# Attention and two expert stages in one kernel: the gate product of the first stage's weights on four column strips, the low parts of w_in on POOL

## The chip, the cores and the metric

The kernel runs on one core of one Trainium2 chip. The metric is device microseconds (us) of that core, from the first to the last instruction of one launch with what lies around it. Three runs of the kernel before gave 736.51, 736.69 and 737.07 us (median 736.69).

The engines are TensorE (PE, its weight loads are PEld), VectorE (DVE), ScalarE (ACT), GpSimd (POOL) and SyncE (SP, which here only issues DMAs). Each works through its own list of instructions in order.

## The reference

All arrays are float32, except that `moe_w_in` and `moe_w_out` (scaled by a float64 number) come as float64.

```python
# attention: q, k, v are (4, 12, 448, 64)
scores = cap * np.tanh(scale * (q @ k.transpose(0, 1, 3, 2)) / cap)
attn = np.exp(scores - scores.max(-1, keepdims=True))
x = (attn / (attn.sum(-1, keepdims=True) + 1e-9)) @ v      # -> (1792, 768)
# first expert stage: w_in (768, 1024), w_out (1024, 768)
h = x @ w_in
solu = h * softmax(h)
ln = (solu - mean(solu)) / np.sqrt(var(solu) + 1e-6) * g_ln
x = ln @ w_out
# second: each row goes to one of 8 experts
logits = x @ w_gate + modality_bias[modality_id]           # w_gate (768, 8)
e = argmax(logits); gate_w = softmax(logits)[e]
out = gate_w * (relu(x @ w1[e]) @ w2[e])
```

## The kernel before

**Early phase.** The 4 x 12 heads are taken as 24 pairs of heads, and a pair as two *units*, so that unit u is half u mod 2 of pair u // 2 (`unit(n, cp)`, L920). In a unit PE makes the scores of two key chunks (`sc`, L740), ACT takes their tanh (L747) and exp (L752), and PE multiplies the exponentials of the unit before with v (`av`, L782) and adds up their sums on four column strips of the array (`S`, L788). A "column strip" is a quarter of the 128 columns of PE's array: a matmul whose stationary operand has 32 columns can be put on one of four.

**Weights of the first expert stage.** Beside this, in units 0 to 13, two blocks of weights a unit are converted: 16 blocks of w_out (128 x 384, chunk c = 0 to 7, half hf = 0, 1) and 12 of w_in (128 x 512, chunk k = 0 to 5). Units 0 to 11 take one of each, units 12 and 13 two of w_out. DVE puts the float64 halves together to float32 with three integer operations (L481 to L483). Then each weight is split into a rounded high part and a low part, since the products run as three passes (high x high, high x low, low x high):

- w_in: ACT casts the high part (`winh`, L518), DVE subtracts it from the whole (`winl`, L519).
- w_out: DVE scales by g_ln for the high part (`wouh`, L533) and for the low part (`woul`, L534).

**Gate columns.** `wouh`/`woul` carry eight more columns: w_out times w_gate, so that the logits come out of the same product. For that, PE transposes each half block (`pt`, L542), ACT copies the transpose out (`wT`, L545), and PE multiplies: six accumulating matmuls with a 128 x 128 piece of `wT` as stationary operand and 8 gate columns moving (`po`, L552). ACT writes the high part of the 128 x 8 result (L553), DVE the low part (L554, the "gate" step).

**What sets the order.** For the first 8 pairs the order of PE, ACT, DVE and SP is that of the code; POOL's is left to a scheduler. Steps are put off in lists that `unit` empties at fixed places (`flush`): `pe` behind the scores, `cast` (the casts of w_in) behind it, `gate` and `sub` behind each conversion on DVE. PSUM tiles `sc`, `pt`, `po`, `h`, `lt`, `y` share three slots (`atile`), so a tile waits until the tile that had its slot three tiles before is read. Float32 blocks (`ti`, `to`) share four slots, raw blocks four.

In the unit that holds `po` of chunk c, PE runs `sc`, `po`, `pt` (c+1, half 0), `av`, `S`; in the next `sc`, `pt` (c+1, half 1), `av`, `S`. The later phase (from pair 8) runs the two expert stages among the remaining attention; its functions are not touched.

Of the kernel before, what the change touches and what calls it, by code (L numbers as in the profile page):

```python
# [22 lines left out]
P = 128  # L23
# [64 lines left out]
def attn_moe_kernel(ctx, tc, qt, kt, vv, w_in, w_out, packed, ids, mbias, w1, w2, out):  # L88
# [17 lines left out]
    cap_t, g_t = pk[:, 0:1], pk[:, 1:1 + NF]  # L106
    wg_t = pk[:, 1 + NF:].rearrange("p (d w) -> p d w", w=NE)
    sc8 = con.tile([P, 1], F32, name="sc8")
# [5 lines left out]
    bias_t = con.tile([P, NTILE, NE], F32, name="bias_t")  # L114
    mhalf = con.tile([P, 16], F32, name="mhalf")[:, :1]
    lg = con.tile([P, NTILE, NE], F32, name="lg")
    gidx = con.tile([P, NG], I32, name="gidx")
# [9 lines left out]
    ga0 = edge.tile([P, 8], F32, name="ga0")[:, :2]  # L127
    nmx = con.tile([P, NTILE], F32, name="nmx")
    gar = con.tile([P, 80], F32, name="gar")
# [342 lines left out]
    def atile(nm):  # L472
        clock.take(nm)
        return psA.tile([P, 2, 512], F32, tag="A", name=nm)
# [9 lines left out]

    later = {"pe": [], "cast": [], "gate": [], "sub": []}

    def flush(kind):
        fs, later[kind] = later[kind], []
        for f in fs:
            f()  # L490
# [18 lines left out]
    def conv_in(k, hf):  # L509
        raw = rawof[True, k, hf]  # L510
        t = mp.tile([P, 512], I32, tag="x3", name=f"ti{k}_{hf}", bufs=4)
        f64_to_f32(t, raw)
        conv_load()
        tf = t.bitcast(F32)
        h_, l_ = winh[k][:, hf * 512:(hf + 1) * 512], winl[k][:, hf * 512:(hf + 1) * 512]

        def cast():
            act.copy(h_, tf)  # L518
            later["sub"].append(lambda: dve.tensor_sub(l_, tf, h_))  # L519

        later["cast"].append(cast)
# [3 lines left out]
    def conv_out(c, hf):  # L525
# [10 lines left out]
        later["pe"].append(lambda: conv_tr(c, hf))  # L536

    def conv_tr(c, hf):
        tf = wT[c, hf]
        pt = atile(f"pt{c}_{hf}")[:, 0, :]  # L540
        for i in range(3):
            pe.transpose(pt[:, i * P:(i + 1) * P], tf[:, i * P:(i + 1) * P], ident)  # L542
        if hf == 0:
            wT[c] = mp.tile([P, YW], F32, tag="ys", name=f"wT{c}", bufs=1)[:, :DM].rearrange("p (a b) -> p a b", b=P)
        act.copy(wT[c][:, 3 * hf:3 * hf + 3, :], pt[:, :3 * P].rearrange("p (a b) -> p a b", a=3))  # L545
        if hf:
            later["pe"].append(lambda: conv_og(c))

    def conv_og(c):
        po = atile(f"po{c}")[:, 0, :]  # L550
        for i in range(ND):
            pe.matmul(po[:, :NE], wT[c][:, i, :], wg_t[:, i, :], start=(i == 0), stop=(i == ND - 1))  # L552
        act.activation(wouh[c][:, DM:YW], po[:, :NE], AF.Copy, scale=g_t[:, c:c + 1])  # L553
        later["gate"].append(lambda: dve.scalar_tensor_tensor(  # L554
            woul[c][:, DM:YW], po[:, :NE], g_t[:, c:c + 1], wouh[c][:, DM:YW], op0=ALU.mult, op1=ALU.subtract))

# [363 lines left out]
    def unit(n, cp):  # L920
        (b, p), u = pairs[n], 2 * n + cp
        a_scp(b, p, cp)
        flush("pe")
        flush("cast")
        early = plain(b, p) and b > 0
        if early and p and not cp:
            flush("gate")
            finish(b - 1, 4 * p)
        a_exp(b, p, cp)
        if early:  # L930
            if p or cp:
                flush("gate")
                flush("sub")
            if not p or cp:
                finish(b - 1, 4 * p + 2 * cp)
        if cp == 0 and n:
            a_av(*pairs[n - 1], chunks=(2, 3))
        elif cp:
            a_av(b, p, chunks=(0, 1))
        fill(FW[0])  # L940
        if b > 0 and not plain(b, p):
# [8 lines left out]
        flush("gate")  # L950
        flush("sub")
        if u == 3:
# [728 lines left out]
```

## Time and profile before

| | |
|---|---|
| median of 3 runs | 736.69 us |
| profiled execution: its time, its span | 736.02 us, 734.2 us |
| granted TensorE clock (mean share of full) | 0.998 |
| PE, DVE, ACT, POOL busy (share of span) | 98%, 60%, 53%, 14% |
| HBM traffic over the span | 131 GB/s |

The profile's numbers are of one execution of 736.02 us, 0.67 us below the median; the span leaves 1.8 us around it. PE is called busy while a matmul is under way, also one that waits in the array; which engine sets the pace in a stretch is read from the waits and the chain. In the early phase, up to some 75 us, DVE, ACT and PE are each busy more than nine tenths of the time, POOL not at all.

### The profile page before, as it was taken

The numbers are of one execution on the slowest core, as the hardware profiler recorded it, in microseconds if no ns is written. First come the engines' busy times: TensorE is split into PE (matmuls) and PEld (weight loads), VectorE is DVE, ScalarE is ACT, GpSimd is POOL, SyncE is SP. The second block draws the span as 40 slices with busy tenths as digits, with TensorE's granted clock in tenths as the row PEclk, the third lists the DMA queues.
The fourth block names the chain that finished last, engine by engine and source line by source line (L and its number), as shares of the span: only waits on it lengthen the run. The fifth ranks groups of instructions, "written<-read, shape, count | busy, mean of one in ns | idle before, by whom it ended". The sixth has DMA issues, their size and how long they took to land.

```text
span 734.2 us, 11333 instructions
## 1 busy us (share of the span) xinstructions
PE 722.2 (98%) x4310; PEld 558.0 (76%) x4310; DVE 438.0 (60%) x785; ACT 387.6 (53%) x536; POOL 103.9 (14%) x187
## 2 busy tenths in 40 slices
PE   8999999999999999999999999999999999999996
PEld 3443557567767778677778999899879998799995
DVE  7999656647666566565366645857246173473632
ACT  7999756775575554665541224345155162553522
POOL 2000101111031020220030311023110220002011
PEclk9999999999999999999999999999999999999999
DMA  8777221121121110110002202488937359673640
GB/s 277 229 246 242 75 63 50 52 64 44 50 85 38 59 60 13 60 35 13 22 1 105 69 23 79 138 277 305 408 115 262 141 169 393 241 234 141 223 163 25
DMA packets 34354, 97.15 MB, mean 132 GB/s; under 512 B 4647, under 2 KB 10933, under 8 KB 34290
## 3 DMA queue, kind: packets, MB, share of 16 engines
q1 hardware_dynamic: 30578, 79.27, 31.9%
q0 software_dynamic: 3568, 16.83, 6.2%
q8 instruction: 36, 0.59, 0.3%
q10 hardware_dynamic: 144, 0.23, 0.1%
q14 instruction: 28, 0.23, 0.1%
HBM read 85.24 MB, written 11.27 MB: 131 GB/s over the span
## 4 chain that ended last, share of the span: by engine, by line
PE 85%; DVE 6%; ACT 2%; issue 2%; DMA 1%; POOL 1%; POOLq 1%; SPq 0%; another core or an unknown queue 0%; DVEq 0%; ACTq 0%
PE av L782 9%; PE sc L740 8%; PE h L598 6%; PE h L599 5%; PE h L601 5%; PE y L654 5%; PE y L657 5%; PE y L655 4%; PE poD L1389 3%; PE poD L1391 3%; PE poD L1390 3%; PE phD L1286 3%; PE phD L1288 3%; PE phD L1287 3%; PE lt L634 1%
## 5 line engine op out<-in xcount | busy, mean ns | idle before, releaser
L747 ACT ACTIVATE e<-sc,sc 112x896 f32<-112x896 f32 x96 | 94.4, 1004 | 57.7 <-PE sc L740 57.6
L752 ACT ACTIVATE e<-e,pk 112x896 f32<-112x896 f32 x96 | 98.2, 1046 | 1.7
L782 PE MATMUL av<-e,v 112*64 112x448 f32 x384 | 82.8, 552 | 0.9 <-DMA v<-in_vv_dram 0.9
L654 PE MATMUL y<-wouh,lh 128*128 128x392 f32 (+1 forms) x224 | 77.7, 347 | 0.0
L655 PE MATMUL y<-woul,lh 128*128 128x392 f32 (+1 forms) x224 | 75.9, 339 | 0.0
L657 PE MATMUL y<-wouh,ll 128*128 128x392 f32 (+1 forms) x224 | 71.5, 339 | 0.2 <-DVE ll L644 0.2
L598 PE MATMUL h<-winh,xh 128*128 128x512 f32 x168 | 68.9, 410 | 0.0
L599 PE MATMUL h<-winl,xh 128*128 128x512 f32 x168 | 65.8, 392 | 0.0
L601 PE MATMUL h<-winh,xl 128*128 128x512 f32 x168 | 61.2, 391 | 0.0
L782 PEld LDWEIGHTS av<-e,v 112*64 112x64 f32 x384 | 23.4, 136 | 36.5 <-issue 33.7
L654 PEld LDWEIGHTS y<-wouh,lh 128*128 128x128 f32 x224 | 42.0, 188 | 8.4 <-issue 7.1
L1230 DVE TENSOR_TENSOR wl_D<-raw_D,wh_D 128x768 fp32r<-128x768 f32 (+1 forms) x28 | 29.9, 1072 | 27.9 <-ACT wh_D L1229 24.8
L598 PEld LDWEIGHTS h<-winh,xh 128*128 128x128 f32 x168 | 31.6, 188 | 16.6 <-issue 10.0
L1389 PE MATMUL poD<-wh_D,hhD 128*128 128x384 f32 x128 | 43.0, 336 | 0.0
L1391 PE MATMUL poD<-wh_D,hlD 128*128 128x384 f32 x128 | 42.8, 334 | 0.0
L1390 PE MATMUL poD<-wl_D,hhD 128*128 128x384 f32 x128 | 42.8, 334 | 0.0
L1230 DVE TENSOR_TENSOR wl_H<-raw_H,wh_H 128x768 fp32r<-128x768 f32 (+1 forms) x28 | 29.2, 1070 | 22.3 <-ACT wh_H L1229 22.3
L655 PEld LDWEIGHTS y<-woul,lh 128*128 128x128 f32 x224 | 42.1, 188 | 0.6
L657 PEld LDWEIGHTS y<-wouh,ll 128*128 128x128 f32 x224 | 41.9, 188 | 0.6 <-DVE ll L644 0.6
L1229 ACT CAST wh_D<-raw_D 128x768 fp32r<-128x768 f32 (+1 forms) x28 | 26.0, 933 | 30.7 <-DMA raw_D<-in_w_dram 30.3
L711 POOL TENSOR_TENSOR kl<-kr,kh 128x448 fp32r<-128x448 f32 x16 | 18.4, 1152 | 144.1 <-ACT kh L710 84.2
L1288 PE MATMUL phD<-xh_D,wl_D 128*128 128x512 f32 x96 | 37.4, 389 | 0.0
(384 smaller groups left out, 1592.9 us busy)
## 6 DMA issues: line engine op xcount, KB each, us to landing
rawc<-in_w_out_dram SPq DMA_DIRECT2D x16, 384.0 KB, 4.0
rawc<-in_w_in_dram SPq DMA_DIRECT2D x12, 512.0 KB, 4.2
raw_D<-in_w_dram SPq DMA_DIRECT2D x12, 512.0 KB, 5.4
wr_T<-in_w_dram SPq DMA_DIRECT2D x16, 384.0 KB, 6.7
raw_D<-in_w_dram SPq DMA_DIRECT2D x16, 384.0 KB, 6.0
wr_T<-in_w_dram SPq DMA_DIRECT2D x12, 512.0 KB, 9.3
raw_H<-in_w_dram SPq DMA_DIRECT2D x12, 512.0 KB, 8.7
raw_H<-in_w_dram SPq DMA_DIRECT2D x16, 384.0 KB, 4.2
```

The lines of the kernel that those rows point to most:

```text
L598: pe.matmul(o, s["xh"][d], winh[d][:, c], start=(d == 0), stop=False)
L599: pe.matmul(o, s["xh"][d], winl[d][:, c], start=False, stop=False)
L601: pe.matmul(o, s["xl"][i], winh[i][:, c], start=False, stop=(i == ND - 1))
L654: pe.matmul(o, s["lh"][f], wouh[f][:, c], start=(f == 0), stop=False)
L655: pe.matmul(o, s["lh"][f], woul[f][:, c], start=False, stop=False)
L657: pe.matmul(o, s["ll"][i], wouh[i][:, c], start=False, stop=(i == NF - 1))
L747: act.activation(e, t[:CK, :, :S], AF.Tanh, scale=sc8[:CK])
L752: act.activation(e, e, AF.Exp, scale=cap_t[:CK])
L782: pe.matmul(o[64 * j:64 * j + 64, :S], v[:, c, 64 * j:64 * j + 64], et[b, p, c][:, j, :], start=(c == 0), stop=(c == 3))
L1389: pe.matmul(p, hh[:, f, o], wh[:, c], start=(f == 0), stop=False)
L1390: pe.matmul(p, hh[:, f, o], wl[:, c], start=False, stop=False)
L1391: pe.matmul(p, hl[:, f, o], wh[:, c], start=False, stop=(f == NF - 1))
```

## The change

Four things are changed, all in the early phase.

1. The gate product has its operands swapped. The stationary operand is now a run of 32 columns out of the 48 gate columns (8 for each of 6 pieces), the moving one a 128 x 128 piece of `wT`. Six such matmuls are spread over the four column strips: strips 0 and 2 take two pieces, strips 1 and 3 one. They stand behind `av` and `S` of the unit that transposes half 1 (`flush("strip")`) and write the second bank of that transpose's own PSUM tile.
2. The four strips are added up by one further matmul: DVE copies the 128 x 128 result to SBUF (`part`, which shares its tile with the later `lg` and `nmx`), and PE multiplies `part` as stationary operand with `gsel`, a 128 x 8 matrix of ones and zeros (`conv_og`). It stands behind the next chunk's first transpose and writes the second bank of that tile. `gsel` is built at the start by three POOL operations on 128 x 8.
3. The low parts of w_in are subtracted on POOL.
4. ACT's cast of w_in comes behind the two exps of the unit, not ahead of them.

```diff
--- before.py
+++ after.py
@@ -104,7 +104,7 @@
     pk = con.tile([P, NPK], F32, name="pk")
     make_identity(nc, ident)
     cap_t, g_t = pk[:, 0:1], pk[:, 1:1 + NF]
-    wg_t = pk[:, 1 + NF:].rearrange("p (d w) -> p d w", w=NE)
+    wg_t = pk[:, 1 + NF:]
     sc8 = con.tile([P, 1], F32, name="sc8")
     epsv = con.tile([P, 1], F32, name="epsv")
     zone = con.tile([CK, 63], F32, name="zone")
@@ -112,8 +112,13 @@
     sel = con.tile([P, NP, P], F32R, name="sel")
     rh = con.tile([P, S], F32R, name="rh")
     bias_t = con.tile([P, NTILE, NE], F32, name="bias_t")
-    mhalf = con.tile([P, 16], F32, name="mhalf")[:, :1]
-    lg = con.tile([P, NTILE, NE], F32, name="lg")
+    few = con.tile([P, 16], F32, name="mhalf")
+    mhalf, gsel = few[:, :1], few[:, 8:16]
+    pool.tensor_tensor(out=gsel, in0=ident[:, 0:NE], in1=ident[:, 32:32 + NE], op=ALU.add)
+    for i in (64, 96):
+        pool.tensor_tensor(out=gsel, in0=gsel, in1=ident[:, i + 24:i + 24 + NE], op=ALU.add)
+    part = con.tile([P, P], F32, name="lg")
+    lg, nmx = part[:, :NTILE * NE].rearrange("p (t e) -> p t e", e=NE), part[:, NTILE * NE:NTILE * NE + NTILE]
     gidx = con.tile([P, NG], I32, name="gidx")
     sidx = con.tile([P, NG], I32, name="sidx")
     eidx = con.tile([1, NS], I32, name="eidx")
@@ -125,7 +130,6 @@
     sidx0 = con.tile([P, 2], I32, name="sidx0")
     edge = ctx.enter_context(tc.tile_pool(name="edge", bufs=1, side="right"))
     ga0 = edge.tile([P, 8], F32, name="ga0")[:, :2]
-    nmx = con.tile([P, NTILE], F32, name="nmx")
     gar = con.tile([P, 80], F32, name="gar")
 
     dve.memset(rh.bitcast(F32), 0.0)
@@ -482,7 +486,7 @@
         dve.scalar_tensor_tensor(dst, hi, -0x40000000, dst, op0=ALU.bitwise_and, op1=ALU.bitwise_or)
         dve.scalar_tensor_tensor(dst, lo, 29, dst, op0=ALU.logical_shift_right, op1=ALU.bitwise_or)
 
-    later = {"pe": [], "cast": [], "gate": [], "sub": []}
+    later = {"pe": [], "cast": [], "strip": [], "gate": []}
 
     def flush(kind):
         fs, later[kind] = later[kind], []
@@ -516,7 +520,7 @@
 
         def cast():
             act.copy(h_, tf)
-            later["sub"].append(lambda: dve.tensor_sub(l_, tf, h_))
+            pool.tensor_sub(l_, tf, h_)
 
         later["cast"].append(cast)
 
@@ -535,24 +539,36 @@
         wT[c, hf] = tf
         later["pe"].append(lambda: conv_tr(c, hf))
 
+    gates = []
+
     def conv_tr(c, hf):
         tf = wT[c, hf]
-        pt = atile(f"pt{c}_{hf}")[:, 0, :]
+        pt = atile(f"pt{c}_{hf}")
         for i in range(3):
-            pe.transpose(pt[:, i * P:(i + 1) * P], tf[:, i * P:(i + 1) * P], ident)
+            pe.transpose(pt[:, 0, i * P:(i + 1) * P], tf[:, i * P:(i + 1) * P], ident)
+        if gates:
+            conv_og(gates.pop(), pt[:, 1, :NE])
         if hf == 0:
             wT[c] = mp.tile([P, YW], F32, tag="ys", name=f"wT{c}", bufs=1)[:, :DM].rearrange("p (a b) -> p a b", b=P)
-        act.copy(wT[c][:, 3 * hf:3 * hf + 3, :], pt[:, :3 * P].rearrange("p (a b) -> p a b", a=3))
+        act.copy(wT[c][:, 3 * hf:3 * hf + 3, :], pt[:, 0, :3 * P].rearrange("p (a b) -> p a b", a=3))
         if hf:
-            later["pe"].append(lambda: conv_og(c))
-
-    def conv_og(c):
-        po = atile(f"po{c}")[:, 0, :]
-        for i in range(ND):
-            pe.matmul(po[:, :NE], wT[c][:, i, :], wg_t[:, i, :], start=(i == 0), stop=(i == ND - 1))
-        act.activation(wouh[c][:, DM:YW], po[:, :NE], AF.Copy, scale=g_t[:, c:c + 1])
+            later["strip"].append(lambda: conv_st(c, pt[:, 1, :P]))
+
+    def conv_st(c, o):
+        for i, g, first, last in ((0, 0, 1, 0), (2, 1, 1, 1), (3, 2, 1, 0), (5, 3, 1, 1), (1, 0, 0, 1), (4, 2, 0, 1)):
+            w = i * NE - (24 if g > 1 else 0)
+            pe.matmul(o[32 * g:32 * g + 32], wg_t[:, w:w + 32], wT[c][:, i, :], start=bool(first), stop=bool(last))
+        later["gate"].append(lambda: dve.tensor_copy(part, o))
+        if c == NF - 1:
+            later["pe"].append(lambda: conv_og(c, atile(f"po{c}")[:, 0, :NE]))
+        else:
+            gates.append(c)
+
+    def conv_og(c, po):
+        pe.matmul(po, part, gsel, start=True, stop=True)
+        act.activation(wouh[c][:, DM:YW], po, AF.Copy, scale=g_t[:, c:c + 1])
         later["gate"].append(lambda: dve.scalar_tensor_tensor(
-            woul[c][:, DM:YW], po[:, :NE], g_t[:, c:c + 1], wouh[c][:, DM:YW], op0=ALU.mult, op1=ALU.subtract))
+            woul[c][:, DM:YW], po, g_t[:, c:c + 1], wouh[c][:, DM:YW], op0=ALU.mult, op1=ALU.subtract))
 
     rpool = []
     X, tail = {}, {}
@@ -921,22 +937,22 @@
         (b, p), u = pairs[n], 2 * n + cp
         a_scp(b, p, cp)
         flush("pe")
-        flush("cast")
         early = plain(b, p) and b > 0
         if early and p and not cp:
             flush("gate")
             finish(b - 1, 4 * p)
         a_exp(b, p, cp)
+        flush("cast")
         if early:
             if p or cp:
                 flush("gate")
-                flush("sub")
             if not p or cp:
                 finish(b - 1, 4 * p + 2 * cp)
         if cp == 0 and n:
             a_av(*pairs[n - 1], chunks=(2, 3))
         elif cp:
             a_av(b, p, chunks=(0, 1))
+        flush("strip")
         fill(FW[0])
         if b > 0 and not plain(b, p):
             finish(b - 1, 4 * p + 2 * cp)
@@ -948,7 +964,6 @@
                 early = False
                 finish(b - 1, 4 * p + 2 * cp + 1)
         flush("gate")
-        flush("sub")
         if u == 3:
             setup_second(*tables)
         a_esp(b, p, cp)
```

On PE, in units 4 and 5: `pt1_1` is the transpose of chunk 1's half 1, `pt2_0` that of chunk 2's half 0, `sc0_2_x` are scores. Before:

```order
L542 MATMUL pt1_1_390<-ident_61,to1_1_348 128x128 x3
L782 MATMUL av0_1_339<-e0_1_2_318,v0_1_217 64x448 x2
L782 MATMUL av0_1_339<-e0_1_3_319,v0_1_217 64x448 x2
L788 MATMUL S0_239<-e0_1_2_318,zone_69 32x448 x2
L788 MATMUL S0_239<-e0_1_3_319,zone_69 32x448 x2
L740 MATMUL sc0_2_2_424<-qr0_2_265,kr0_2_263 112x448 x2
L740 MATMUL sc0_2_3_427<-qr0_2_265,kr0_2_263 112x448 x2
L552 MATMUL po1_434<-pk_62,wT1_334 128x8 x6
L542 MATMUL pt2_0_442<-ident_61,to2_0_407 128x128 x3
```

Now, at the same place:

```order
L548 MATMUL pt1_1_393<-ident_61,to1_1_352 128x128 x3
L798 MATMUL av0_1_343<-e0_1_2_327,v0_1_219 64x448 x2
L798 MATMUL av0_1_343<-e0_1_3_328,v0_1_219 64x448 x2
L804 MATMUL S0_242<-e0_1_2_327,zone_69 32x448 x2
L804 MATMUL S0_242<-e0_1_3_328,zone_69 32x448 x2
L560 MATMUL pt1_1_393<-wT1_337,pk_62 32x128 x6
L756 MATMUL sc0_2_2_434<-qr0_2_267,kr0_2_265 112x448 x2
L756 MATMUL sc0_2_3_437<-qr0_2_267,kr0_2_265 112x448 x2
L548 MATMUL pt2_0_444<-ident_61,to2_0_417 128x128 x3
L568 MATMUL pt2_0_444<-mhalf_74,lg_78 128x8
```

The six matmuls of `po` have left the place ahead of `pt2_0`; six on strips stand ahead of the scores, and one stands behind `pt2_0`.

On DVE, from the conversion of chunk 2's half 0 (`to2_0`) to that of half 1 (`to2_1`). Before:

```order
L533 TENSOR_SCALAR wouh2_130<-to2_0_407,pk_62 128x384
L534 SCALAR_TENSOR_TENSOR woul2_138<-to2_0_407,pk_62,wouh2_130 128x384
L481 TENSOR_SCALAR ti2_0_415<-rawc9_307 128x512
L482 SCALAR_TENSOR_TENSOR ti2_0_415<-rawc9_307,ti2_0_415 128x512
L483 SCALAR_TENSOR_TENSOR ti2_0_415<-rawc9_307,ti2_0_415 128x512
L519 TENSOR_TENSOR winl1_123<-ti1_1_357,winh1_117 128x512
L481 TENSOR_SCALAR to2_1_460<-rawc10_352 128x384
```

Now (`lg_78` is the tile that holds `part`):

```order
L537 TENSOR_SCALAR wouh2_132<-to2_0_417,pk_62 128x384
L538 SCALAR_TENSOR_TENSOR woul2_140<-to2_0_417,pk_62,wouh2_132 128x384
L561 COPY lg_78<-pt1_1_393 128x128
L485 TENSOR_SCALAR ti2_0_426<-rawc9_317 128x512
L486 SCALAR_TENSOR_TENSOR ti2_0_426<-rawc9_317,ti2_0_426 128x512
L487 SCALAR_TENSOR_TENSOR ti2_0_426<-rawc9_317,ti2_0_426 128x512
L485 TENSOR_SCALAR to2_1_465<-rawc10_356 128x384
```

The subtraction is gone from DVE's list, and the copy of `part` stands behind the conversion of w_out in every second unit. The order of the later phase is the same on every engine.

## Rows read from the trace of the kernel before

**Rows 1.** The page: shares of the chain that ended last, by engine.
```profile
PE 85%; DVE 6%; ACT 2%; issue 2%; DMA 1%; POOL 1%; POOLq 1%; SPq 0%; another core or an unknown queue 0%; DVEq 0%; ACTq 0%
```
**Rows 2.** Busy time by stretch: length, engines' busy us (instructions), clock, DMA share.
```profile
6.70:36.60 29.90, 27.72 (x168) 11.03 (x164) 28.56 (x64) 28.14 (x40) 0.00 (x0) 1.00 0.82 269
36.60:75.20 38.60, 38.60 (x238) 16.41 (x238) 36.67 (x72) 35.93 (x52) 0.00 (x0) 1.00 0.75 244
```
**Rows 3.** The chain in order of time (start us, us, what), around 36.6 us.
```profile
36.40 0.15 DVE woul L554
36.59 0.55 PE pt L542 x3
```
**Rows 4.** PE's instructions in time: start us, us, line, output<-inputs, count.
```profile
30.95 0.52 PE L542 MATMUL pt<-ident,to 128*128 128x128 f32 x3
...
63.06 1.51 PE L552 MATMUL po<-pk,wT 128*128 128x8 f32 x12
64.42 0.53 PE L542 MATMUL pt<-ident,to 128*128 128x128 f32 x3
64.88 1.72 PE L782 MATMUL av<-e,v 112*64 112x448 f32 x8
66.53 0.96 PE L788 MATMUL S<-e,zone 112*32 112x448 f32 x8
67.42 1.76 PE L740 MATMUL sc<-qr,kr 64*112 64x448 f32 x8
69.11 0.55 PE L542 MATMUL pt<-ident,to 128*128 128x128 f32 x3
...
75.18 0.53 PE L542 MATMUL pt<-ident,to 128*128 128x128 f32 x3
...
93.90 0.50 PE L598 MATMUL h<-winh,xh 128*128 128x512 f32 x1
```
**Rows 5.** DVE's instructions in time, in the same columns.
```profile
31.36 0.42 DVE L481 TENSOR_SCALAR ti<-rawc 128x512 int32<-128x512 int32 x1
...
46.37 0.22 DVE L554 SCALAR_TENSOR_TENSOR woul<-po,pk,wouh 128x8 fp32r<-128x8 f32 x1
...
48.30 0.68 DVE L519 TENSOR_TENSOR winl<-ti,winh 128x512 fp32r<-128x512 f32 x1
48.90 0.35 DVE L481 TENSOR_SCALAR to<-rawc 128x384 int32<-128x384 int32 x1
...
56.45 0.22 DVE L554 SCALAR_TENSOR_TENSOR woul<-po,pk,wouh 128x8 fp32r<-128x8 f32 x1
...
71.61 0.36 DVE L481 TENSOR_SCALAR to<-rawc 128x384 int32<-128x384 int32 x1
```
**Rows 6.** POOL's subtraction of k and DVE beside it, in time.
```profile
205.30 1.14 POOL L711 TENSOR_TENSOR kl<-kr,kh 128x448 fp32r<-128x448 f32 x1
...
205.60 1.79 DVE L766 TENSOR_TENSOR es<-es,e 112x896 f32<-112x896 f32 x1 [0.31 <-ACT e L752]
...
295.73 1.15 POOL L711 TENSOR_TENSOR kl<-kr,kh 128x448 fp32r<-128x448 f32 x1
...
295.83 1.99 DVE L765 TENSOR_TENSOR es<-es,e 112x896 f32<-112x896 f32 x1
...
297.93 1.09 DVE L766 TENSOR_TENSOR es<-es,e 112x896 f32<-112x896 f32 x1
```
**Rows 7.** POOL's short product beside a DVE operation, and one with DVE idle.
```profile
116.42 0.75 DVE L619 TENSOR_SCALAR u<-u,sm 128x1024 f32<-128x1024 f32 x1
...
116.56 0.67 POOL L624 TENSOR_TENSOR sm<-sm 128x1 f32<-128x1 f32 x1
...
231.24 0.19 POOL L624 TENSOR_TENSOR sm<-sm 128x1 f32<-128x1 f32 x1
```
**Rows 8.** Groups by line: output<-inputs, shapes, count, busy us, mean ns, idle before.
```profile
L711 POOL TENSOR_TENSOR kl<-kr,kh 128x448 fp32r<-128x448 f32 x16 | 18.4, 1152 | 144.1 <-ACT kh L710 84.2 <-PE sc L740 42.1 <-DVE kh L710 17.5
...
L836 DVE TENSOR_TENSOR tail<-X,rb 128x128 f32<-128x128 f32 x3 | 0.9, 286 | 0.2 <-PE rb L830 0.2
```

## The prediction

> **What bounds the kernel now.** I read the page's shares of the chain first [rows 1]: 85% of the span hangs on PE, 6% on DVE. That mean says little of this change, which lies wholly in the first 94 of 734.2 us. So the second view is the busy time by stretch [rows 2]. From 6.7 to 36.6 us DVE is busy 28.56 of 29.90 us, ACT 28.14, PE 27.72; from 36.6 to 75.2 us PE all of 38.60, DVE 36.67, ACT 35.93. POOL has nothing to do in either. The reader is to see three engines within a tenth of each other: taking work from one gives little unless the next can follow.
>
> Third comes the chain in order of time [rows 3]: up to 36.55 us it is DVE's unbroken row of conversions, and there PE's transpose waits for DVE's gate step; from then on the chain is PE. Fourth is one pair of units on PE [rows 4] and on DVE [rows 5]. PE needs 75.18 - 36.59 = 38.59 us from the transpose of chunk 2, half 1 to that of chunk 6, half 0, which is 3.5 pairs. DVE needs 56.45 - 46.37 = 10.08 us a pair, from gate step to gate step; in it are two subtractions at 0.60 (48.30 to 48.90), the rest is conversion.
>
> **The change part by part.**
>
> *Gate product on PE.* `po` takes 64.42 - 63.06 = 1.36 us of PE [rows 4]. No row shows four strips with 128 moving columns. The nearest is `S`: four matmuls of 448 columns, one on each strip, take 67.42 - 66.53 = 0.89 us, so 128 columns take 0.25 a round. Strips 0 and 2 run two rounds: 0.50 us, which I take. The ends are 0.34 (a quarter of 1.36) and 1.36 (nothing runs side by side). The final matmul with 8 moving columns is one of six like those of `po`: 1.36 / 6 = 0.23. So PE gains 1.36 - 0.50 - 0.23 = 0.63 us a chunk (ends 0.79 and -0.23), 5.0 us over eight chunks if nothing else held it.
>
> The Trainium skill (TensorEngine Tiling (Array Packing), Stationary-Streaming Swap + Column Tiling) promises up to four times for this very swap where the moving dimension is 32 or less. By it the six matmuls would take the lower end, 0.34, and the sum below would not move, since PE does not set it.
>
> *DVE.* The twelve subtractions leave: 12 x 0.60 = 7.2 us. Eight copies of 128 x 128 out of PSUM come; the nearest row is a 128 x 128 product with a PSUM operand, 0.286 us [rows 8], so 0.3 each and 2.4 in all (ends 0.2, near the 128 x 8 gate step of 0.22 [rows 5], and 0.6).
>
> *POOL.* Its subtraction of 128 x 448 takes 1.152 us [rows 8] and an operation of one column 0.19 [rows 7]; that is 2.15 ns a column, and 1.29 us for 512 (an estimate). POOL is idle, so its own time costs nothing. But the trace shows that POOL and DVE hold each other up. DVE's sum of two tiles takes 1.09 us alone [rows 6]; started 0.30 us after a POOL subtraction it took 1.79 (held 0.70), started 0.10 us after one it took 1.99 (held 0.90). Both ended as if they had begun 0.14 us before POOL's end. It goes the other way too: POOL's short product takes 0.19 us with DVE idle and 0.67 beside DVE's one-input operation, ending as that one does [rows 7]. The conversions on DVE are of these two kinds, two tiles in or one tile at a fast rate, and DVE is hardly ever idle up to 75 us.
>
> What would a POOL subtraction of 1.29 us hold? At most 1.29 - 0.14 = 1.15, at least nothing, if it falls into a gap or beside a copy from PSUM (`tail<-X,rb` type). The rows give 0.70 and 0.90 for one that is 0.14 shorter; some of it falls beside the copy and the gate step (0.30 + 0.22, some 0.5 us a pair) or beside DVE's own waits. I take 0.75: 12 x 0.75 = 9.0 us. So DVE's list grows by 2.4 + 9.0 - 7.2 = 4.2 us, and each subtraction moved costs DVE 0.15 instead of freeing 0.60. DVE rises from 10.08 a pair to 10.08 - 1.20 + 0.30 + 1.50 = 10.68, about PE's old pace.
>
> The Trainium skill states the mechanism (SBUF — State Buffer, Who interferes with whom): a DVE instruction with two SBUF inputs, or in a two-port mode, and a GpSimd instruction that reads SBUF exclude each other for the whole instruction, and whichever starts first wins. The trace agrees, with 0.70 and 0.90 us held. Taken to the letter, with every subtraction holding all of 1.29 us, DVE would take 11.8 us a pair.
>
> *New waits.* The copy of `part` stands behind a w_out conversion on DVE, and the next chunk's first transpose on PE takes the slot of the tile from which it is copied. Behind that transpose queue the gate matmul, `av`, `S` and the next scores, and ACT waits for those. So PE now needs DVE in every pair at this place. The cast behind the exps is the same ACT work; ACT keeps 38.60 - 35.93 = 2.67 us free [rows 2], just above the 2.5 that PE gains there. The cast's readers (POOL, then DVE two units later) have several us. Three POOL operations for `gsel` lie in POOL's idle time.
>
> *The sum, at three places.*
> 1. Transpose of chunk 2, half 0 (30.95 us). DVE ends the conversion ahead of it at 31.36 [rows 5], later than PE asks: before, only the first operations of that block were needed. Ahead of this point are three subtractions, two copies and three POOL subtractions: 31.36 - 1.80 + 0.60 + 2.25 = 32.4. From there PE runs `pt` 0.45, gate matmul 0.23, `av` and `S` 2.54, scores 1.69 to the next transpose: 37.35, against 36.59 before. Late by 0.8.
> 2. Transpose of chunk 6, half 0 (75.18). DVE's block ahead of it ends at 71.61, 40.25 after 31.36. In between are eight subtractions, four copies, eight POOL subtractions: 40.25 - 4.80 + 1.20 + 6.00 = 42.65, so 32.4 + 42.65 = 75.05. PE alone would be there at 37.35 + 38.59 - 4 x 0.63 = 73.4. So DVE is late last, and the place comes at 75.1: 0.1 gained.
> 3. The first `h` (93.90). Two more `po` leave (2.72); three gate matmuls and two strip groups come (0.69 + 1.00): 1.0 gained. But two transposes a unit, sums and reciprocals share the three slots here, and tiles are held longer, until DVE has copied or run the gate step. I keep half, 0.4 with the rounding on the safe side (ends 0 and 1.0).
>
> Sum: -0.1 - 0.4 = -0.5 us. Behind `h` all engines' lists are as before, so the shift stays. The profiled execution of 736.02 becomes 735.5; as it lies 0.67 below the median, the forecast in terms of the median is 736.69 - 0.5 = 736.2 us. A difference within 0.2% (1.5 us) can't be told from none.
>
> **The rivals.**
>
> *DVE is hardly held.* POOL's subtractions fall into gaps or wait. For: POOL can be made to wait [rows 7]. Against: DVE's row has hardly a gap, and DVE was held in both rows 6. With nothing held, place 1 is PE's own, 30.95 - 0.63 = 30.3, place 2 comes at 30.3 + 4.9 + 38.59 - 2.5 = 71.3, 3.9 early, and with 0.6 of place 3 it is 4.5: 732.2 us.
>
> *Held by half, about 0.5 us each.* Place 1 at 31.65, place 2 for DVE at 75.05 - 11 x 0.25 = 72.3, for PE 72.6: 2.6 early, with 0.5 of place 3 3.1: 733.6 us.
>
> *Slower: DVE held longer.* POOL waits for a running DVE operation, then holds the next one for nearly its whole length. One mechanism, at place 2: at 0.95 us each, 11 x 0.20 = 2.2 is added, so +2.1 - 0.4 = +1.7: 738.4. It decides from about 0.93 us held on, where the sum passes +1.5. For: the row with a start 0.10 us after POOL's, 0.90 for a shorter subtraction. At 1.15 it would be +3.9.
>
> *The strips run one after another.* Then PE loses 0.23 a chunk: place 2 at 37.35 + 0.86 + 38.59 + 0.9 = 77.7, +2.5, and 0.7 at place 3: 739.9 us. Against: `S`, whose four strips take 0.89 us while `av`, with 64 columns a tile on two strips, takes 66.53 - 64.88 = 1.65 for as many matmuls [rows 4].
>
> **How the numbers follow.** Forecast (held 0.65 to 0.92 us) 0.42; hardly held 0.17; held by half 0.19; held longer 0.15; strips in a row 0.07. The forecast's own range is 11 x 0.10 to 11 x 0.17 about 736.2: 735.1 to 738.1. The range for 8 in 10 reaches from the foot of the first rival to just above the slower one: 732.2 to 738.6. Faster by over 0.2%: 0.17 + 0.19 and nothing from the forecast's edge, 0.36; slower: 0.15 + 0.07, 0.22; within: 0.42.
>
> **What would show it.** In the changed profile POOL should show twelve subtractions of 1.25 to 1.5 us between 14 and 80 us, and beside each a conversion on DVE that takes 0.6 to 1.0 us more than its like (0.42 becoming 1.1 or more for the first operation on a w_in block). DVE's gate steps should lie 10.4 to 11 us apart. The strips should take about 0.5 us and start within some 0.02 us on the four strips. PE's first transpose of a chunk should be found waiting for DVE, where before it was not. `h` should start within 1.5 us of 93.90. I am wrong if DVE's conversions keep their lengths while POOL subtracts, if the strips' records lie 0.1 us apart, or if the difference arises behind `h`.

## The result and the profile after

| | before | after |
|---|---|---|
| median | 736.7 us | 741.9 us (741.22 to 743.43) |
| ratio after / before, 95% | | 1.0070 [1.0059, 1.0080] |
| profiled execution: time, span | 736.02, 734.2 us | 742.75, 741.0 us |
| first `h` on PE | 93.90 us | 99.82 us |

The kernel became slower by 0.7%, or 5.2 us. The forecast was 736.2 us, its range 732.2 to 738.6. Of the 6.7 us between the two profiled executions some 1.5 are scatter: before was profiled 0.67 us below its median, after 0.85 above its own. Nearly all of it is there when the first `h` starts (5.92 us); 0.9 us arises behind it and is not traced. From the first `h` to the end the kernel before takes 640.3 us, the kernel after 641.2, and the other kernels of this document between 640.3 and 642.1, so these 0.9 us can't be told from scatter. One of the six executions of the kernel before in this comparison took 892.51 us and is left out of the median and the ratio.

The busy times by stretch, in the columns of [rows 2]:

```profile
6.70:36.60 29.90, 23.52 (x155) 9.24 (x153) 28.11 (x56) 25.70 (x36) 5.45 (x4) 0.99 0.74 244
36.60:75.20 38.60, 36.89 (x239) 13.61 (x239) 36.85 (x63) 34.67 (x49) 10.29 (x7) 0.96 0.68 224
75.20:93.90 18.70, 16.56 (x124) 7.97 (x122) 14.41 (x32) 12.95 (x21) 2.05 (x2) 0.91 0.32 99
```

In [rows 2] PE was busy for 27.72 and 38.60 us of the first two stretches; now it has holes, while DVE is as busy as before. The clock column, 1.00 before, reads 0.96 and 0.91: for a part of the time PE ran at the lower of its two levels (1.2 of 2.4 GHz), which is 0.50 in this column. PE's waits from 6 to 100 us (engine, tile and line, who ended the wait, us in total, times, the longest) name the engine that it waits for:

```profile
PE pt L548 <- DVE lg L561: 7.5, 5, 3.7
PE pt L548 <- DVE to L487: 1.3, 2, 0.9
```

L561 is the copy of `part` (the trace calls its tile `lg`). PE in time at the prediction's place 1, the row at 34.75 answering to that at 30.95 in [rows 4]:

```profile
34.75 0.55 PE L548 MATMUL pt<-ident,to 128*128 128x128 f32 x3 [3.68 <-DVE lg L561]
35.13 0.29 PE L568 MATMUL pt<-mhalf,lg 128*128 128x8 f32 x2
35.35 2.43 PE L798 MATMUL av<-e,v 112*64 112x448 f32 x8
37.71 1.72 PE L804 MATMUL S<-e,zone 112*32 112x448 f32 x8
...
44.08 0.61 PE L560 MATMUL pt<-wT,pk 128*32 128x128 f32 x12
44.61 0.63 PE L756 MATMUL sc<-qr,kr 64*112 64x448 f32 x2
```

Two things stand here. PE waits 3.68 us for the copy of `part`. And the work behind the wait is slow: `av` takes 2.43 us and `S` 1.72, where [rows 4] have 1.72 and 0.96 for the same shapes; the granted clock is 0.75 from 34.7 to 37.8 us and 0.50 from 37.8 to 39.5. The strips themselves (44.08 to 44.61) take 0.53 us and the gate matmul 0.22, as forecast.

Why the copy is late is seen where POOL and DVE run side by side, in time:

```profile
14.54 1.27 POOL L523 TENSOR_TENSOR winl<-ti,winh 128x512 fp32r<-128x512 f32 x1 [8.27 <-ACT winh L522]
14.72 1.64 DVE L486 SCALAR_TENSOR_TENSOR ti<-rawc,ti 128x512 int32<-128x512 int32 x1
...
19.09 1.27 POOL L523 TENSOR_TENSOR winl<-ti,winh 128x512 fp32r<-128x512 f32 x1 [3.28 <-ACT winh L522]
19.10 1.67 DVE L538 SCALAR_TENSOR_TENSOR woul<-to,pk,wouh 128x384 fp32r<-128x384 f32 x1
...
25.39 1.36 DVE L485 TENSOR_SCALAR ti<-rawc 128x512 int32<-128x512 int32 x1
...
29.95 1.27 POOL L523 TENSOR_TENSOR winl<-ti,winh 128x512 fp32r<-128x512 f32 x1 [3.48 <-ACT winh L522]
30.01 1.24 DVE L181 TENSOR_SCALAR tmp<-tmp 128x14 f32<-128x14 f32 x1
...
34.41 0.28 DVE L561 COPY lg<-pt 128x128 f32<-128x128 f32 x1
34.61 0.41 DVE L485 TENSOR_SCALAR ti<-rawc 128x512 int32<-128x512 int32 x1
```

The DVE operation that starts beside a subtraction takes 1.64 us instead of 0.69, 1.67 instead of 0.62; in these two it ends as if it had begun 0.14 and 0.21 us before POOL's end. All twelve subtractions do this to one DVE operation each: seven with two inputs (L486, L538) and five with one (L485, L181). The time by which an operation is lengthened is called a hold here. The sums stand in DVE's groups by line and shape, 6.7 to 93.9 us (columns as in [rows 8]):

```profile
L538 DVE SCALAR_TENSOR_TENSOR woul<-to,pk,wouh 128x384 fp32r<-128x384 f32 x16 | 13.8, 862 | 0.6
L486 DVE SCALAR_TENSOR_TENSOR ti<-rawc,ti 128x512 int32<-128x512 int32 x12 | 11.2, 930 | 0.4
...
L485 DVE TENSOR_SCALAR ti<-rawc 128x512 int32<-128x512 int32 x12 | 8.8, 731 | 0.0
...
L561 DVE COPY lg<-pt 128x128 f32<-128x128 f32 x8 | 2.3, 283 | 2.6 <-PE pt L560 2.6
```

Unheld, these and the small operation of L181 (above, at 30.01) take 0.62, 0.69, 0.42 and 0.17 us. So, by the means, 16 x (0.862 - 0.62), 12 x (0.930 - 0.69), 12 x (0.731 - 0.42) and 1.24 - 0.17 make 3.9 + 2.9 + 3.7 + 1.1 = 11.6 us of holds, 0.96 each (0.88 to 1.07) where 0.75 was taken. A copy of `part` takes 0.28 us, but the next operation starts 0.20 us after it (34.41 to 34.61), so the copies lengthen DVE's list by 8 x 0.20 = 1.6 us. In all it grows by 11.6 + 1.6 - 7.2 = 6.0 us.

Last, PE from place 2 to the first `h` (75.18 and 93.90 in [rows 4]):

```profile
79.01 0.55 PE L548 MATMUL pt<-ident,to 128*128 128x128 f32 x3 [0.87 <-DVE lg L561]
...
80.56 0.85 PE L548 MATMUL pt<-ident,to 128*128 128x128 f32 x3 [0.87 <-DVE to L487]
81.33 3.03 PE L798 MATMUL av<-e,v 112*64 112x448 f32 x8
...
99.82 0.50 PE L614 MATMUL h<-winh,xh 128*128 128x512 f32 x1
```

A second wait comes 1.5 us behind the first, and behind both `av` takes 3.03 us.

### The profile page after: what moved, and what is told of

It is laid out like the page before. It is cut to its first block, busy times and chain, and to the rows that moved or that the text cites. A ratio compares the mean times of both kernels' runs of the same rounds, so it can differ in the third digit from the quotient of the medians.

```text
span 741.0 us, 11383 instructions
## 1 busy us (share of the span) xinstructions
PE 720.1 (97%) x4326; PEld 554.0 (75%) x4326; DVE 443.2 (60%) x781; ACT 386.8 (52%) x536; POOL 121.7 (16%) x202
## 5 line engine op out<-in xcount | busy, mean ns | idle before, releaser
L798 PE MATMUL av<-e,v 112*64 112x448 f32 x384 | 84.8, 563 | 0.8 <-DMA v<-in_vv_dram 0.8
L798 PEld LDWEIGHTS av<-e,v 112*64 112x64 f32 x384 | 23.7, 137 | 36.4 <-issue 33.0
L1302 PE MATMUL phD<-xl_D,wh_D 128*128 128x512 f32 x96 | 37.4, 389 | 0.0
## 6 DMA issues: line engine op xcount, KB each, us to landing
wr_T<-in_w_dram SPq DMA_DIRECT2D x12, 512.0 KB, 10.2
```

Of the source, the lines that this page charges most:

```text
L798: pe.matmul(o[64 * j:64 * j + 64, :S], v[:, c, 64 * j:64 * j + 64], et[b, p, c][:, j, :], start=(c == 0), stop=(c == 3))
```

## The experiments

Theory A: GpSimd's subtractions hold DVE, DVE's lateness becomes PE's waits, and the clock falls behind these. Rival B: the strips' scheme is slow in itself. Rival C: only the place of the copy of `part` matters. Twelve kernels were run, each timed against the kernel before. Differences in us are differences of ratios times 736.7.

| kernel | subtraction | gate product | copy of `part` | median us | ratio, 95% | first `h` |
|---|---|---|---|---|---|---|
| before | DVE | `po` | - | 736.7 | 1 | 93.90 |
| cast late | DVE | `po` | - | 736.5 | 1.0000 [0.9992, 1.0009] | 93.72 |
| POOL sub alone | POOL | `po` | - | 743.9 | 1.0093 [1.0078, 1.0109] | 100.68 |
| after | POOL | strips | DVE | 741.9 | 1.0070 [1.0059, 1.0080] | 99.82 |
| strips, DVE sub | DVE | strips | DVE | 735.8 | 0.9994 [0.9985, 1.0003] | 93.36 |
| copy on ACT | POOL | strips | ACT | 739.1 | 1.0037 [1.0025, 1.0049] | 96.65 |
| both | DVE | strips | ACT | 733.7 | 0.9962 [0.9948, 0.9975] | 91.86 |

**1. Strips with the subtraction on DVE.**

```diff
-            pool.tensor_sub(l_, tf, h_)
+            later["sub"].append(lambda: dve.tensor_sub(l_, tf, h_))
# and flush("sub") behind flush("gate"), as before the change
```

> The changed kernel with the subtraction of w_in put back on VectorE (the strips, the copy of `part` and the late cast stay). Theory A (the subtractions on GpSimd hold VectorE's instructions, 12 holds of 0.96 us in the trace of the changed kernel, and TensorE's clock falls after the waits that this brings): VectorE's operations beside the old places of the subtractions are back at 0.2 to 0.7 us, TensorE waits under 1 us ahead of the transposes of chunk 2 instead of 3.68, the scores' part av x8 at 35 us takes 1.72 us instead of 2.43, and the time is 0.5 to 2 us below the kernel before: 735 to 736.5. Rival B (the strips' scheme is itself slow: VectorE's copy of `part` is a new wait of TensorE and ScalarE): the wait ahead of the transposes stays over 2 us and the time stays at least 2 us above the kernel before, 739 to 742.

Measured 735.8: theory A's time, 5.6 us under the kernel after, though not told from the kernel before (0.9985 to 1.0003). But two of A's details failed, as PE's rows in time show:

```profile
32.50 0.90 PE L548 MATMUL pt<-ident,to 128*128 128x128 f32 x3 [2.38 <-DVE lg L561]
...
33.56 2.87 PE L798 MATMUL av<-e,v 112*64 112x448 f32 x8
```

The wait for the copy of `part` is still 2.38 us and `av` still slow. So that wait does not need the holds, and there is something in rival B, which the next runs size.

**2. The subtraction on POOL alone.**

```diff
-            later["sub"].append(lambda: dve.tensor_sub(l_, tf, h_))
+            pool.tensor_sub(l_, tf, h_)
```

> The kernel before with one part of the change alone: the 12 subtractions of w_in on GpSimd, behind the cast at its old, earlier place; the gate product as it was. Theory A (holds of VectorE by GpSimd): each of the 12 subtractions holds one VectorE operation for 0.9 to 1.05 us where one of VectorE's own took 0.6, so VectorE is up to 12 x 0.36 = 4.3 us later over the stretch, and the time is 2 to 5 us above the kernel before: 739 to 742. Rival B (the strips and their copies are what costs): VectorE loses no more than it saves, the time is within 1 us of the kernel before or under it.

743.9: 6.9 us slower, more than A had room for. With no strips in it, this single edit accounts for the whole of the change's loss and more. PE in time waits for DVE's gate step, and `av` behind takes 3.26 us:

```profile
39.79 1.84 PE L740 MATMUL sc<-qr,kr 64*112 64x448 f32 x4 [2.47 <-DVE woul L554]
41.56 0.90 PE L542 MATMUL pt<-ident,to 128*128 128x128 f32 x3
42.39 3.26 PE L782 MATMUL av<-e,v 112*64 112x448 f32 x8
```

At the `S` behind this `av`, PE is 6.85 us behind the kernel before (45.57 against 38.72), and at the first `h` still 6.78: no further wait for DVE lies between. The granted clock is 0.50 from 39.7 to 45.6 us, so about half of these 5.9 us, some 3 us, is the lower clock (an estimate); 0.65 is a later first raw block, and the rest is DVE's lateness.

**3 and 4. The copy of `part` on ACT**, first in the kernel after, then in kernel 1.

```diff
-        later["gate"].append(lambda: dve.tensor_copy(part, o))
+        later["gate"].append(lambda: act.copy(part, o))
```

> The changed kernel with the copy of `part` on ScalarE in place of VectorE; the subtractions stay on GpSimd. Theory A (VectorE's lateness by the holds is what TensorE waits for, whichever of its instructions stands last): the wait ahead of the transposes of chunk 2 is then put down to VectorE's fold of w_out or its gate step, and stays at 2.5 to 3.7 us; the time moves by less than 1.5 us against the changed kernel (740.5 to 742). Rival C (the new wait is the PSUM slot that the copy of `part` holds, a matter of where that copy stands in VectorE's order): the wait goes under 1 us and the time falls by 3 us or more, to 737 to 739.

> Both at once: subtraction on VectorE, copy of `part` on ScalarE; the strips stay. Theory A: no holds and 8 copies of 0.28 us fewer on VectorE, no lower clock ahead of the first h; 1.5 to 3 us below the kernel before, 734 to 735.5, if VectorE is the engine that TensorE waits for in this stretch. Rival B (the strips themselves are slow): 739 or more. Rival D (ScalarE is then the late one): within 0.7 us of the kernel with the subtraction on VectorE and the copy on VectorE.

The first gave 739.1, 2.4 us under the kernel after: between A's and C's numbers, and right for neither. PE's row at place 1:

```profile
33.67 0.52 PE L548 MATMUL pt<-ident,to 128*128 128x128 f32 x3 [1.89 <-DVE to L487]
...
34.24 1.72 PE L798 MATMUL av<-e,v 112*64 112x448 f32 x8
```

The wait is halved, it is now for the conversion itself, and `av` runs at full speed. The second gave 733.7, 2.8 us under the kernel before as A said (1.5 to 3), and 8.0 under the kernel after. Rival D, with ScalarE late, falls too. PE in time:

```profile
31.76 0.55 PE L548 MATMUL pt<-ident,to 128*128 128x128 f32 x3
...
37.21 0.55 PE L548 MATMUL pt<-ident,to 128*128 128x128 f32 x3 [0.55 <-DVE woul L570]
...
91.86 0.50 PE L614 MATMUL h<-winh,xh 128*128 128x512 f32 x1
```

The parts now add up: strips with the copy on ACT -2.8, the copy on DVE +2.4 (with the subtraction on either engine), the subtraction on POOL +5.6 or +5.5; together +5.2. Rival B falls: the strips gain, though it was right that the copy of `part` on DVE is dear. Rival C falls as well: with the copy off DVE the subtraction on POOL still costs 5.5 us.

**5. The late cast alone** (`flush("cast")` behind `a_exp`, in the kernel before).

> The kernel before with one part of the change alone: the cast of w_in behind the exps; subtraction on VectorE, gate product as it was. All theories: next to nothing, 736 to 738 against 736.6. If it costs 2 us or more, the lateness of the changed kernel is partly the cast's place; if it gains over 1 us, then part of what the strips' version with the subtraction on VectorE gained (735.8) is the cast's.

736.5, no difference. In the fastest kernel, with the cast put back ahead of the exps, none either: 734.3, ratio 0.9969 [0.9957, 0.9981].

> The fastest kernel so far (strips, subtraction on VectorE, copy of `part` on ScalarE; 733.7) with the cast of w_in back at its earlier place, ahead of the exps. The cast's place alone made no difference in the kernel before (736.5 against 736.5); expected the same here: 733 to 734.5. If TensorE's waits for ScalarE's exps are now what ends last, the earlier cast makes each exp 0.5 us later and the time 735 or more.

**6 and 7. What on POOL holds DVE.** In the kernel after, other POOL instructions in place of the subtraction:

```diff
-            pool.tensor_sub(l_, tf, h_)
+            pool.memset(tf, 0.0)                 # kernel 6
+            pool.memset(l_.bitcast(F32), 0.0)
+            pool.tensor_scalar(l_, tf, 0.0, None, op0=ALU.mult)   # kernel 7
```

> The changed kernel with two memsets on GpSimd (of the fold's tile and of the low part) in place of each subtraction; so the low parts of w_in are left out of the result. The memsets read nothing from SBUF and write the same tiles. Theory A1 (what holds VectorE is GpSimd's reading of two operands of SBUF): VectorE's operations beside them take 0.2 to 0.7 us, VectorE is 12 x 0.96 = 11.5 us less busy, TensorE's wait of 3.68 goes under 2.5, the time is 735 to 737, near the kernel with the subtraction on VectorE (735.8) or under it. Rival A2 (any instruction of GpSimd on SBUF holds VectorE for as long as it runs): the operations beside them are longer by nearly the memsets' duration, and the time is 740 or more.

> The changed kernel with a one-operand instruction on GpSimd in place of the subtraction (the low part becomes 0 x the fold, so the low parts of w_in are left out of the result): it reads one tile of SBUF and writes one. If only two operands read by GpSimd hold VectorE (theory A1), VectorE's operations beside it are at 0.2 to 0.7 us and the time is 735 to 737. If every reading or writing of GpSimd holds it (A2), the holds are the instruction's duration less 0.3 us and the time follows: at a duration of 1.1 to 1.3 us 740 to 742, at one of 0.6 us some 737 to 739.

Kernel 6 gave 735.9, ratio 0.9992 [0.9984, 1.0001]. The memsets of `tf`, 0.52 to 0.82 us each, lengthen no DVE operation with two inputs beside them, as A1 has it, and PE's wait of 3.68 us is down to 0.57. But the memsets of the low part waited for nothing and ran early, ten of them in a row, and DVE's first operation, with one input (0.36 us elsewhere), stood against all of them:

```profile
6.22 4.72 POOL L524 MEMSET winl<- 128x512 f32 x10
```

```profile
6.90 4.25 DVE L485 TENSOR_SCALAR to<-rawc 128x384 int32<-128x384 int32 x1 [2.76 <-DMA rawc<-in_w_out_dram]
```

So A1 does not hold for that operation, DVE's list starts 3.9 us late, and the kernel's time says little. Kernel 7 is the cleaner one: 734.3, ratio 0.9967 [0.9954, 0.9980], 7.6 us under the kernel after. POOL and DVE in time:

```profile
10.98 1.55 POOL L523 TENSOR_SCALAR winl<-ti 128x512 fp32r<-128x512 f32 x1 [4.71 <-DVE ti L487]
11.19 0.85 DVE L486 SCALAR_TENSOR_TENSOR to<-rawc,to 128x384 int32<-128x384 int32 x1
12.07 0.56 DVE L487 SCALAR_TENSOR_TENSOR to<-rawc,to 128x384 int32<-128x384 int32 x1
```

POOL's instruction is longer than the subtraction (1.55 against 1.27 us), yet DVE's is only 0.29 us longer (0.85 against 0.56), the same beside eleven of the twelve. It also no longer waits for ACT's cast, and so starts at another place in DVE's list; but the DVE operation behind its start is again an L486 with two inputs, 0.21 us later, as in the pair at 14.54 and 14.72 above (0.18 later, held 0.95). Twelve times 0.96 - 0.29 is 8.0 us less on DVE, and 7.6 came out. A1 holds in its main point. The Trainium skill (SBUF — State Buffer, Who interferes with whom) has a DVE instruction with two SBUF inputs fully blocked by a GpSimd instruction that reads SBUF and started first; the seven operations with two inputs beside the subtractions agree, held for 0.88 to 1.06 us. The one-input instruction of kernel 7 reads SBUF too and blocked such operations for 0.28 to 0.30 us only, so there the measurement differs from the Trainium skill, as far as the profile's rough spans on POOL show it.

**8 to 11. What the lower clock costs.** Extra matmuls were to keep PE at work through a wait. In the kernel after, ahead of the transposes of chunk 2:

```diff
+        if (c, hf) == (2, 0):
+            for _ in range(14):        # 30 in the second attempt
+                pe.matmul(spt[0][:, 448:512], ident, ident[:, :64], start=False, stop=False, ...)
```

> The changed kernel with 14 extra matmuls (ident on ident, 128 columns, into a part of a PSUM tile that nobody reads) in front of the transposes of chunk 2, so that TensorE works during most of its wait of 3.68 us; by the transposes' 0.18 us each they take some 2.6 us. Theory A (the 2.43, 1.72 and 1.88 us behind that wait are a lower granted clock, and what TensorE did before decides it): av x8 takes 1.72, S 0.96, sc 1.76, TensorE is 1.6 us earlier at 41 us; of these 1.6 us between nothing (VectorE is as late as before and the next waits grow by as much) and all comes through: 740.3 to 742 against 741.9. Rival E (these matmuls are slow for another reason, their operands or PSUM ports): they stay at 2.43, 1.72 and 1.88 and the time stays within 0.5 us.

> The changed kernel with 30 extra matmuls of 64 columns (ident on ident) ahead of the transposes of chunk 2, this time into columns of the scores' sum bank that nobody reads, so that they need not wait for VectorE's copy of `part`, as the 14 of the first attempt did. Theory A: they run within the wait of 3.68 us, av x8 behind it takes 1.72 instead of 2.43, S 0.96 instead of 1.72, and the time is 740.3 to 742 against 741.9, depending on how much of the 1.6 us the next waits for VectorE take back. Rival E: 2.43 and 1.72 stay, and the time stays within 0.5 us.

> The changed kernel with 14 extra matmuls of 64 columns (ident on ident) ahead of the transposes of chunk 2, less than half of the 30 before, which took 6.91 us and so ran 2.3 us past the end of the wait; 14 take some 3.2 us and end within it. Theory A (the fall of the clock is a loss of its own): av x8 behind the wait takes 1.72, S 0.96, the first h comes 1 to 1.6 us earlier than 99.8, and the time is 740.3 to 741. Theory F (VectorE's sum of work sets the pace of this stretch, and the fall of the clock only fills time in which TensorE would wait for VectorE anyway, as in the fastest kernel, where the cure of the first fall brought nothing): av x8 takes 1.72 too, but the next waits for VectorE grow, the first h stays within 0.7 us of 99.8, and the time is 741.2 to 742.5.

The first attempt, 14 of 128 columns, wrote into a part of the tile of which `part` is copied, so its matmuls stood behind the same wait: 744.3, ratio 1.0113 [1.0097, 1.0130]. PE in time:

```profile
35.14 4.73 PE L548 MATMUL pt<-ident 128*128 128x128 f32 x28 [3.10 <-DVE lg L565]
...
40.26 1.72 PE L802 MATMUL av<-e,v 112*64 112x448 f32 x8
```

The wait was not filled, and the granted clock is 0.50 from 35.1 to 37.5 us: the fall now lies on the extra matmuls, and `av` behind them is at full speed. The second attempt wrote elsewhere, but I had sized 30 of them at half their cost: they took 6.91 us and ran 2.3 us past the wait: 743.9, ratio 1.0105 [1.0089, 1.0120]; no wait was left, the clock stayed at 1.00, and `av` took 1.72 us. With 14 the wait is filled (the trace counts each of them twice). PE in time:

```profile
31.72 3.34 PE L548 MATMUL S<-ident 128*128 128x64 f32 x28
...
35.49 1.72 PE L801 MATMUL av<-e,v 112*64 112x448 f32 x8
...
39.73 0.55 PE L551 MATMUL pt<-ident,to 128*128 128x128 f32 x3
...
45.82 0.55 PE L551 MATMUL pt<-ident,to 128*128 128x128 f32 x3 [0.88 <-DVE lg L564]
...
80.65 1.72 PE L801 MATMUL av<-e,v 112*64 112x448 f32 x8
...
97.83 0.50 PE L617 MATMUL h<-winh,xh 128*128 128x512 f32 x1
```

PE is 1.44 us earlier at 39.73 (41.17 in the kernel after), waits 0.88 for DVE at 45.82 where there was no wait, and is 0.35 earlier at place 2 (78.66 against 79.01). So three quarters of the first fall were under DVE's cover, as theory F says (two thirds, if one allows for DVE's first operation, which starts 0.21 us later in this execution). The second fall did not come here, worth 1.6 us from 80.65 on, so the first `h` is 1.99 us earlier, more than F's 0.7 and than A's 1.6. It is not the filling alone: of four profiles with the same two waits of 0.87 to 0.90 us there, the second fall comes in two (the kernel after and the second attempt, `av` 3.03 and 3.07 us) and not in two (the first attempt and this one). This is also the quickest execution of five (740.46 to 741.86). The median, 741.4, ratio 1.0068 [1.0055, 1.0082], is F's, and not told from the kernel after.

The same cure for the first `av` of the fastest kernel, 10 such matmuls:

> The fastest kernel so far (733.7) with 10 extra matmuls of 64 columns (ident on ident, into columns of the scores' sum bank that nobody reads) ahead of its first av x8, where TensorE waits 1.26 us for the load of v and then takes 2.84 us for av x8 and 1.49 for S, against 1.72 and 0.96 at the full granted clock. Theory A (the clock falls for want of work ahead of it): av x8 takes 1.72, S 0.96, and TensorE is 1.6 us earlier at 15 us; what of that comes through is between nothing (VectorE sets the pace) and all: 732 to 733.7. Rival E (the slow matmuls have another cause, the load of v itself among them): 2.84 and 1.49 stay and the time is 733.7 to 734.5.

PE in time, first in the fastest kernel without the extra matmuls, then in the same kernel with the early cast (`flush("cast")` ahead of the exps, also without them), then with them:

```profile
10.78 2.84 PE L798 MATMUL av<-e,v 112*64 112x448 f32 x8 [1.26 <-DMA v<-in_vv_dram]
```

```profile
10.78 1.72 PE L798 MATMUL av<-e,v 112*64 112x448 f32 x8 [1.31 <-ACT e L763]
```

```profile
9.35 2.34 PE L794 MATMUL S<-ident 128*128 128x64 f32 x20
11.62 1.72 PE L801 MATMUL av<-e,v 112*64 112x448 f32 x8
...
37.15 0.55 PE L548 MATMUL pt<-ident,to 128*128 128x128 f32 x3 [1.24 <-DVE woul L570]
```

With the extra matmuls `av` takes 1.72 us, but so it does without them in the second row, behind a wait of 1.31 us. The other profiles have 1.72 to 1.90 us for this `av` too, but for kernel 6 with its late start (2.38). So this run doesn't show that filling this wait cures anything. It does show how little the fall was worth: PE stands at its transpose at 37.15 as against 37.21, having waited 1.24 instead of 0.55 for DVE, and the first `h` comes at 91.74 with the filling, at 91.69 with the early cast and at 91.86 behind the fall. 733.9, ratio 0.9962 [0.9948, 0.9975]: no gain.

Rival E falls by the three kernels ahead of this one, in the kernel after: where the wait stayed, the slow time moved to the extra matmuls, and where they filled it, the clock stayed at 1.00. What PE did before decides the clock, though not alone: equal waits are followed by a fall in one execution and not in another.

## Why the prediction was wrong

By the first `h`, the prediction has 93.90 - 0.5 = 93.4 and the trace 99.82: 6.4 us. They split by the prediction's own places.

**Place 1: 32.4 forecast, 34.75 measured.** The first raw block landed 0.59 us later (DVE starts at 7.31, not 6.72); over all profiled runs this start lay between 6.32 and 7.76 us, with `po` and with strips, so I don't put it to the change. The failed step is "I take 0.75": the term was mis-sized, and one hold was left out. Four subtractions lie ahead of this place, not three, since the fourth starts at 29.95 and holds a small operation of the tables (L181, 1.24 us). Their holds are 0.95 + 1.05 + 0.94 + 1.07 = 4.0 us against 2.25: 1.75 more. 32.4 + 0.59 + 1.75 = 34.74. (The copies cost DVE's list 0.20 and not 0.3 each, so the last tenths of this agreement are luck.)

**Place 2: 75.1 forecast, 79.01 measured.** Taking 34.75 as given, the prediction's own sum with 0.96 for a hold is 40.25 - 4.80 + 1.20 + 8 x 0.96 = 44.33; the trace has 44.26. Here too it helps that 0.30 for a copy is too much by 0.10 while DVE once stood idle for 0.29 us (at 44.80). DVE's pace, from gate step to gate step, answers to [rows 5]:

```profile
50.33 0.22 DVE L570 SCALAR_TENSOR_TENSOR woul<-pt,pk,wouh 128x8 fp32r<-128x8 f32 x1
...
61.43 0.22 DVE L570 SCALAR_TENSOR_TENSOR woul<-pt,pk,wouh 128x8 fp32r<-128x8 f32 x1
```

11.10 us in this pair and 10.92 in the next (to 72.35), where the forecast was 10.68 and the sum with 0.96 gives 11.10. So the step that DVE's list, and not PE's, sets place 2 was right. The slower rival had named the size ("about 0.95 each") and got 0.15; the row for it, 0.90 us, was the nearest by its start: there DVE followed POOL by 0.10 us [rows 6], here by 0.18 and 0.01 in the first two. But its sum, 738.4 us, falls short of 741.9 as well, since it priced neither what follows at place 3 nor the clock. I averaged over gaps and copies into which a hold might fall. None fell so: DVE is hardly ever idle, and POOL's subtraction becomes ready when ACT's cast ends, while DVE is inside a conversion.

**Place 3: 18.3 forecast from place 2 to `h`, 20.81 measured.** The prediction priced no wait for a conversion here. The transpose of chunk 6, half 1, now waits 0.87 us for one; before the change DVE had it ready 2.7 us early (73.16 against 75.86, in the rows of the kernel before):

```profile
72.60 0.56 DVE L483 SCALAR_TENSOR_TENSOR to<-rawc,to 128x384 int32<-128x384 int32 x1
```

```profile
75.86 0.55 PE L542 MATMUL pt<-ident,to 128*128 128x128 f32 x3
```

Then `av` takes 3.03 us at the lower clock (granted 0.55 from 81.3 to 84.3 us): the stretch takes 97.83 - 78.66 = 19.17 us where the clock stays up, 1.64 less than 20.81. 18.3 + 0.87 + 1.64 = 20.81. That the clock would fall behind PE's new waits stood nowhere in the prediction.

**What was right.** Strips, gate matmul and copy (0.53, 0.22, 0.28 us for 0.50, 0.23, 0.3); the late cast at nothing; POOL's duration (1.27 unheld, up to 1.66 where POOL waits, for 1.29); the new wait of PE at the tile of `part`, which the prediction named without asking what it costs: +2.4 us, against 1.6 us by which the copies lengthen DVE's list; kernel 1's profile also has a fall of the clock there (0.56 from 32.5 to 36.4 us), and how the 2.4 us split is open. "Wrong if the difference arises behind `h`" applies to 0.9 us at most.

**What stays open.** In the timed pairs the subtraction costs 5.5 to 6.9 us. DVE's sum for it, the holds less 7.2 us, is 11.6 - 7.2 = 4.4 in the kernel after, 10.8 - 7.2 = 3.6 with the subtraction on POOL alone, and 10.2 - 7.2 = 3.0 with the copy on ACT. Of what lies beyond it, 1.2, 3.3 and 2.5 us, the falls of the clock can hold 1.6 in the first (the second fall, which does not come in every execution) and 3 in the second, but this is argued from one profile each. With the copy on ACT no fall is seen, and there the 2.5 us are not assigned.

## What to carry to other kernels

An instruction moved to POOL is not free when DVE has no gaps: price it as the hold (here 0.96 us) against what it took on DVE (0.60), at the full overlap unless the rows show the gaps into which it will fall. Where two engines are within a tenth of each other, add up the change of the later engine's list and expect it to come out nearly whole, and ask of each new wait which engine could do its last small step instead: the copy of `part` on ACT, with the subtraction left on DVE, made the loss of 5.2 us a gain of 2.8. A fall of the clock behind a wait matters where no later wait absorbs it: in the kernel after three quarters of one were absorbed, in the kernel with the subtraction alone on POOL nothing was.

## What the hardware showed that was not expected

- A one-input POOL instruction of 1.53 to 1.55 us held DVE's two-input operation for 0.29 us, a two-input one of 1.27 us held such operations for 0.88 to 1.06.
- Ten memsets in a row on POOL held one DVE operation with one input for 3.9 us (4.25 for 0.36); single memsets did nothing to DVE operations with two inputs.
- Behind waits of 3.68, 2.38 and 2.47 us the same `av` took 2.43, 2.87 and 3.26 us, with a granted clock down to 0.50; where the wait of 3.68 us was filled with matmuls it took 1.72, the granted clock of the stretch 1.00. That is PE at the lower of its two levels (1.2 of 2.4 GHz) for a part of the time. Short waits were not followed by the same thing each time: two waits of 0.87 to 0.90 us close together had a fall behind them in two profiles and none in two others, and behind a wait of 1.89 us with the copy on ACT `av` took 1.72.
